# A retention layer with a gated FFN on one core: the order of all engines is replaced, and the first three FFN units become 128 tokens wide

## The chip, the cores and the metric

The kernel runs on one core of one Trainium2 chip. The metric is the device time of one execution in microseconds, and "time" below is the median of several executions. A core has TensorE (PE, matmuls, with weight loads as PEld), VectorE (DVE), ScalarE (ACT), GpSimd (POOL) and SyncE (SP), which here issues nearly all DMAs. The engines work side by side, each through its own list of instructions in order, and wait for each other with semaphores.

## The reference

Attention by a decaying state (retention), whose output is the input of an FFN with a convolved gate:

```python
# B, H, S, D = 4, 8, 768, 64;  d_model 512, d_ff 1024, three taps
gamma = 1.0 - 2.0 ** (-5.0 - np.arange(H))
for t in range(S):
    state = gamma[None, :, None, None] * state + np.einsum('bhd,bhe->bhde', k[:, :, t], v[:, :, t])
    y[:, :, t] = scale * np.einsum('bhd,bhde->bhe', q[:, :, t], state)
x = y.transpose(0, 2, 1, 3).reshape(B, S, H * D)
h = np.maximum(x @ w_in, 0.0)
conv_out = sum(conv_w[k] * hp[:, k:k + S, :] for k in range(3))   # hp: h padded by one token at each end
out = (h * 1.0 / (1.0 + np.exp(-conv_out))) @ w_out
```

All inputs are float32, and w_in, w_out and conv_w arrive as 64-bit words whose bits the kernel turns into float32 itself.

## The kernel before

The four batches are two groups of two, and a sequence is cut into 12 chunks of 64 tokens. So there are 24 **steps** n, each one chunk of one group: 2 batches, 8 heads, 64 tokens. A step has these tasks.

- `load_qk(n)`, `load_kv(n)`: 512 KB each into the buffer `rw`, of which there are four. A qk load waits until the step that had the buffer is done; the kv load of the same step waits for no buffer of its own.
- `scale_q(n)` on VectorE (L387) and the scaling of v, on ScalarE for the first steps (`scale_v_act`, L399) and on VectorE for the others (`scale_v`, L393). Both multiply by powers of gamma, from the table `gq_sb` (loaded once, 256 KB) or from `gq` tiles that ScalarE makes of it (L381).
- `scores(n)`: 16 products of 64x64 by 64x64 in f32, for steps 0 to 2 as tasks of their own. `masked(n)` (L444, VectorE) applies the causal mask.
- `mix(n)` on TensorE (L424): up to 64 such products, namely the step's outputs y (32), the state's update (16) and the scores of step n+1 (16), two of the one kind and two of the other in turn. Mix 0 has 32, mix 1 has 48.
- `carry(n)` (L452, ScalarE) copies the state for the next step; `x_head(n)` (L468, ScalarE) and `x_rest(n)` (L473, VectorE) split y into two f32r parts, which are the FFN's x; `halo` copies single columns between neighbouring units.

The FFN works in **units** of consecutive steps (`UNITS`, eight of three). A unit of three steps has 2 x 192 tokens, and with an edge column at each end of both batches its x has 388 columns. For each of eight slices f of d_ff, `mm1(u, f)` is 12 f32r matmuls (L553, three products of parts for each quarter of d_model) into `ps_m`; then `relu` (L560) and the middle tap (L568) on ScalarE, the two side taps on VectorE (L573). For each pair p of slices follow the sigmoid (L578, ScalarE), the gating (L583, VectorE) and the split of the result (L587 ScalarE, L592 VectorE). `mm2(u, t, p)` (L605) is 6 matmuls of 512 columns for 128 tokens t and pair p; the last 128 tokens of all are split into two halves of 256 columns. `put` (L613) copies to SBUF, and `out` stores.

Weights: each of the 8 + 8 pieces `w(i)` of 512 KB is loaded (`load_w`, waits for no buffer) and converted by a chain of seven tasks, `w_abs`, `w_clamp`, `w_shift`, `w_sign`, `w_bits`, `w_head`, `w_rest`, mostly on VectorE. `CONV` is the number of conv_w, which takes the first five of them.

What sets the order: `ORDER` holds a string for each engine, one letter a task (s scores, a mix, A to I mm1 of unit 0 to 8, o mm2). `plan` takes the letters in order, keeps a clock with fixed costs for tasks and loads, gives out buffers by it, and emits the tasks; each engine then runs them in just that order. The clock has one more effect: where it shows TensorE waiting for more than 0.7 us ahead of the first mm1, `keep_warm` puts dummy matmuls of 512 columns (L351) there, one for each 232 ns beyond 0.4 us; eight stand at the start in any case. The loads have eight semaphores in turn, so up to eight can be under way.

Of the kernel before, what the change touches and what calls it, by code (L numbers as in the profile page):

```python
# [27 lines left out]
CONV = 2 * NF  # L28
# [5 lines left out]
HALF = (slice(0, D), slice(D, P))  # L34


UNITS = [3, 3, 3, 3, 3, 3, 3, 3]
FIRST_STEP = [sum(UNITS[:u]) for u in range(len(UNITS))]
UNIT_OF = [u for u, w in enumerate(UNITS) for _ in range(w)]
W_MAX = max(UNITS)  # L40
LAST = (len(UNITS) - 1, UNITS[-1] - 1)


EARLY, V_ON_ACT = 2, 10

BUFS = {'rw': 4, 'xu': 3, 't2': 4, 'hc': 11, 'g': 3, 'ps_s': 1, 'ps_yo': 4, 'ps_m': 2, 'gq': 2}


ORDER = {
    "PE": (  # L50
        "sssaaaaAAaAAaAaAaBBaBABaABBBoaoaaBDCCaoDoooCCCCaoDooCooooCaDoooooDooooooDEaaoDEoDoooEoEoooEooaooEoooEFao"
        "EoooFoFaooooaoFooFoFFGFooooooGoGGaaGoooGGooHooooooHHoHoGoHoHooHoooooooooHoooooooooooooo"
    ),
    "DVE": (
        "qqmcqmmhgbqcrhgcbmqhrrlqrlgcbhgmqlbchlmcghbcglbmhqrgcqlbmcrhhgrgbqblyymyzzmqcchqgbyhvlyzvgdcybqmylzzlrre"
        "hzdgzbmrvrqmcelrdyvzqrhgmqyycbzdhclzhgygcyzrzybevbemcdzhhllyggqvbebydzzylzmlreyydezzydyyymqdyzzzzvydyvdq"
        "yzyyezqzdzzvrezmyydrezdyqezmzydqezyreyzzymedzdvrvyzdyevmqvqzeyyrzezmremryyzyvdzdeezyyyzzyydzyzzzeymdddry"
        "yeyyzrzeedzzdezyzyzeyyzyzzdyydzedzydyezzyezdeeyzde"
    ),
    "ACT": (  # L60
        "kavkvcaxvacwxvxcwkxchhavAwawaAaxcvwkAvAcaxwvacAxhkwhvAtcttwaaBatcBgtBvkBxAwttewAxBtxagkcgttxechaBhaBwxxB"
        "ectaDCgtwkgxtgDweaCctCwtCCCetwwxgtgetttCpptepcgCtttcDgtDghekttxtgepepgheDkgDttpEcxcDxDeEtttEegttegEppthc"
        "gxeEgthpEEFtetxcEFextctepgptxhgFFFehFFpettctttFtppGgpeGttGGgcggexxttGteeGgGgHepHtpHGtettHHtgHtgtegetpHtg"
        "eegtppepHtgepppp"
    ),
    "Pool": (
        "xxxxxxxx"
    ),
    "DMA": (
        "qqgwqvvqwvwvqwqvqwvwwqvqwwvqvwwqwqvvvwwqqwvwvwqqvqvvqvooqoqvoqvqvqvooovooqvoooooooooooooooo"  # L70
    ),
}

# [1 line left out]
LETTER = {  # L75
# [5 lines left out]
}  # L81
# [6 lines left out]
def letter(k):  # L88
    if k[0] in ("mm1", "relu"):
        return chr(ord("A") + k[1])  # L90
    return LETTER[k[0]][k[3] // 2 if k[0] == "conv_side" else 0]


# [20 lines left out]
def list_tasks():  # L114
# [14 lines left out]
    for n in range(N_STEPS):  # L129
        c, u = n % NC, UNIT_OF[n]  # L130
        first, width = FIRST_STEP[u], UNITS[u]
        own, both = n <= EARLY, EARLY < n + 1 < N_STEPS
# [37 lines left out]

    for u, width in enumerate(UNITS):
        n0, n1 = FIRST_STEP[u], FIRST_STEP[u] + width
# [35 lines left out]
def plan(tasks):  # L208

    queues = {engine: {} for engine in ORDER}  # L210
    for k, t in tasks.items():
        queues[t[0]].setdefault(letter(k), []).append(k)
# [473 lines left out]
```

## Time and profile before

| | before |
|---|---|
| time, median of 3 runs | 357.53 us (354.54 to 358.0) |
| the profiled execution, its time | 357.53 us |
| its span | 355.8 us |
| TensorE busy, matmuls | 341.0 us (96%), 4349 |
| VectorE busy | 220.8 us (62%) |
| ScalarE busy | 193.3 us (54%) |
| keep-warm matmuls | 37, 13.5 us busy |
| moved by DMA | 40.83 MB, 33.91 read |

The span is the time from the first to the last instruction that the profiler recorded; the execution's own time is 1.73 us longer. A group of instructions has its busy time, the mean of one in nanoseconds, and the idle time of the engine just ahead of it with what ended it. Matmuls overlap in time, so the mean of one is more than its share of the time; where the pace of a run of matmuls is needed, it is read from the chain, which gives start and duration of each run. "issue" is a wait that no semaphore, engine or DMA in the profile explains.

### The profile page before, as it was taken

Reading aid. Unit: us, or ns where it says so; the run is one execution under the profiler, and the core shown is the slowest. Engines: PE = TensorE matmul, PEld = TensorE weight load, DVE = VectorE, ACT = ScalarE, POOL = GpSimd, SP = SyncE. Lnnn points to the kernel's source line nnn. Section 1 sums busy time; section 2 is a strip of 40 time slices with the busy share of each in tenths; the row PEclk is TensorE's granted clock in tenths of the full one; section 3 lists DMA queues with packets and bytes.
Section 4 is the critical chain, followed back from the end, with each engine's and each line's share of the span. In section 5 each row is a group of like instructions: output and inputs, shape, how many; then the busy total and the mean of one; then the engine's idle time right before and its main releaser. Section 6 shows DMA issues by size and latency. Waiting matters only on the chain.

```text
span 355.8 us, 9805 instructions
## 1 busy us (share of the span) xinstructions
PE 341.0 (96%) x4349; PEld 304.5 (86%) x4349; DVE 220.8 (62%) x363; ACT 193.3 (54%) x390; POOL 1.9 (1%) x10
## 2 busy tenths in 40 slices
PE   8789959999999999998999999999999999999994
PEld 6678859998999989887988888889989988998883
DVE  1677956899999959966057745344516831188530
ACT  2865939788657565775163541343627631177422
POOL 1000000000000000000000000000000000000000
PEclk9989999999999999999999999999999999999999
DMA  7979666864830017004300633020020000100202
GB/s 292 412 263 358 214 226 216 320 247 171 298 123 0 4 38 196 34 31 123 117 2 0 186 142 122 2 61 2 29 59 33 0 2 29 29 2 29 88 2 89
DMA packets 13338, 40.83 MB, mean 115 GB/s; under 512 B 1744, under 2 KB 2000, under 8 KB 13296
## 3 DMA queue, kind: packets, MB, share of 16 engines
q1 hardware_dynamic: 13232, 40.14, 32.4%
q8 instruction: 34, 0.56, 0.7%
q0 software_dynamic: 64, 0.07, 0.1%
q14 instruction: 8, 0.07, 0.1%
HBM read 33.91 MB, written 6.29 MB: 113 GB/s over the span
## 4 chain that ended last, share of the span: by engine, by line
PE 96%; issue 2%; DVE 0%; ACT 0%
PE ps_m L553 39%; PE ps_yo L605 38%; PE ps_s L424 6%; PE ps_yo L424 5%; PE ps_st L424 4%; PE ps_yo L351 3%; DVE rw L444 0%; ACT rw L452 0%; ACT t L613 0%; DVE warm L344 0%
## 5 line engine op out<-in xcount | busy, mean ns | idle before, releaser
L553 PE MATMUL ps_m<-xu,w 128*128 128x388 f32 x768 | 144.8, 342 | 1.6 <-issue 1.6
L553 PEld LDWEIGHTS ps_m<-xu,w 128*128 128x128 f32 x768 | 136.8, 189 | 5.8 <-issue 2.1
L605 PE MATMUL ps_yo<-w,g 128*128 128x512 f32 (+1 forms) x600 | 140.2, 386 | 0.0
L605 PEld LDWEIGHTS ps_yo<-w,g 128*128 128x128 f32 x600 | 108.5, 188 | 21.7
L573 DVE SCALAR_TENSOR_TENSOR hc<-hc,cw_sb,hc 128x384 f32<-128x384 f32 x128 | 74.1, 615 | 35.7 <-ACT hc L568 35.4
L560 ACT ACTIVATE hc<-ps_m 128x388 f32<-128x388 f32 x64 | 31.5, 493 | 57.9 <-PE ps_m L553 57.9
L424 PE MATMUL ps_yo<-rw 64*64 64x64 f32 x1472 | 50.3, 223 | 6.3 <-issue 6.3
L424 PEld LDWEIGHTS ps_yo<-rw 64*64 64x64 f32 x1472 | 46.7, 138 | 6.9 <-issue 6.9
L592 DVE TENSOR_TENSOR g<-hc,g 128x768 fp32r<-128x768 f32 x32 | 30.5, 955 | 22.7 <-ACT g L587 22.6
L583 DVE TENSOR_TENSOR hc<-hc,hc 128x768 f32<-128x768 f32 x32 | 30.5, 955 | 14.6 <-ACT hc L578 14.6
L578 ACT ACTIVATE hc<-hc 128x768 f32<-128x768 f32 x32 | 26.9, 845 | 19.8 <-DVE hc L573 19.8
L568 ACT ACTIVATE hc<-hc,cw_sb 128x384 f32<-128x384 f32 x64 | 37.5, 614 | 0.1
L444 DVE TENSOR_TENSOR rw<-ps_s,mask_sb 128x512 f32<-128x512 f32 x24 | 16.6, 690 | 31.9 <-PE ps_s L424 31.9
L587 ACT CAST g<-hc 128x768 fp32r<-128x768 f32 x32 | 26.6, 833 | 14.4 <-PE ps_yo L605 11.5
L424 PEld LDWEIGHTS ps_s<-rw 64*64 64x64 f32 x768 | 24.3, 134 | 7.0 <-issue 5.3
L613 ACT COPY t<-ps_yo 128x512 f32<-128x512 f32 (+1 forms) x25 | 14.2, 568 | 27.1 <-PE ps_yo L605 26.1
L424 PE MATMUL ps_s<-rw 64*64 64x64 f32 x768 | 27.6, 221 | 0.3
L424 PE MATMUL ps_st<-rw 64*64 64x64 f32 x704 | 25.7, 221 | 0.7 <-ACT rw L452 0.7
L424 PEld LDWEIGHTS ps_st<-rw 64*64 64x64 f32 x704 | 23.1, 137 | 1.0 <-ACT rw L452 0.8
L468 ACT CAST xu<-ps_yo 128x512 fp32r<-128x512 f32 x24 | 14.2, 594 | 15.5 <-PE ps_yo L424 12.6
L473 DVE TENSOR_TENSOR xu<-ps_yo,xu 128x512 fp32r<-128x512 f32 x24 | 16.3, 687 | 7.5 <-ACT xu L468 7.4
L452 ACT COPY rw<-ps_st 128x512 f32<-128x512 f32 x22 | 12.9, 587 | 13.4 <-PE ps_st L424 8.9
(30 smaller groups left out, 149.3 us busy)
## 6 DMA issues: line engine op xcount, KB each, us to landing
rw<-in_qk SPq DMA_DIRECT2D x24, 512.0 KB, 4.0
rw<-in_kv SPq DMA_DIRECT2D x24, 512.0 KB, 5.8
w<-in_w_in SPq DMA_DIRECT2D x8, 512.0 KB, 7.3
w<-in_w_out SPq DMA_DIRECT2D x8, 512.0 KB, 6.7
out_y<-t SPq DMA_DIRECT2D x15, 256.0 KB, 2.0
out_y<-t SPq DMA_DIRECT2D x18, 128.0 KB, 2.4
gq_sb<-in_gq SPq DMA_DIRECT2D x1, 256.0 KB, 5.0
gvf_sb<-in_gvf POOLq DMA_DIRECT2D x1, 36.0 KB, 4.3
```

Of the source, the lines that this page charges most:

```text
L424: nc.tensor.matmul(out, lhsT, rhs, start=start, stop=stop, skip_group_check=True)
L444: nc.vector.tensor_tensor(out=heads_of(n)[:, 1], in0=s_of(n), in1=mask_sb.unsqueeze(1).unsqueeze(1).broadcast_to([P, G, NPAIR, C]), op=ALU ...
L473: nc.vector.tensor_tensor(out=lo, in0=y_of(n), in1=hi.bitcast(F32), op=ALU.subtract)
L553: nc.tensor.matmul(buf("ps_m", (u, f))[:, :n], w[:, k], x[:, k], start=(i == 0), stop=(i == len(products) - 1))
L560: nc.scalar.activation(h, buf("ps_m", (u, f))[:, : G * (UNITS[u] * C + 2)], AF.Relu)
L568: nc.scalar.activation(cv, h, AF.Copy, scale=w)
L573: nc.vector.scalar_tensor_tensor(out=cv, in0=h, scalar=w, in1=cv, op0=ALU.mult, op1=ALU.add)
L578: nc.scalar.activation(cv, cv, AF.Sigmoid)
L583: nc.vector.tensor_tensor(out=cv, in0=h, in1=cv, op=ALU.mult)
L587: nc.scalar.copy(g_of(u, p)[:, 0], cv_of(u, 2 * p))
L592: nc.vector.tensor_tensor(out=lo, in0=cv_of(u, 2 * p), in1=hi.bitcast(F32), op=ALU.subtract)
L605: nc.tensor.matmul(ps, g, w[:, cs], start=(f == 0 and i == 0), stop=(f == NF - 1 and i == 2))
```

## The change

`UNITS` becomes two, two, two and then six of three steps: nine units, the first three with 2 x 128 tokens, or 260 columns of x. `V_ON_ACT` goes from 10 to 8, so v of steps 8 and 9 is scaled by VectorE. The strings of all engines are new. `letter` gives the tasks of conv_w letters of their own, so that a string can place them apart from the other weights. Buffers, costs and code of the tasks stay as they are; the lines behind `letter` move down by two.

```diff
-UNITS = [3, 3, 3, 3, 3, 3, 3, 3]
+UNITS = [2, 2, 2, 3, 3, 3, 3, 3, 3]
...
-EARLY, V_ON_ACT = 2, 10
+EARLY, V_ON_ACT = 2, 8
...
     "PE": (
-        "sssaaaaAAaAAaAaAaBBaBABaABBBoaoaaBDCCaoDoooCCCCaoDooCooooCaDoooooDooooooDEaaoDEoDoooEoEoooEooaooEoooEFao"
...
+        "sssaaaaAAAaAAaAABBBBBAaBBCCoCBaCCoaCoCaoCooooDDaaDoooaaoDooDaoDooDEoaoEDoEEaooooaoooEooEoooooEooEFaFFFFF"
...
     "DMA": (
-        "qqgwqvvqwvwvqwqvqwvwwqvqwwvqvwwqwqvvvwwqqwvwvwqqvqvvqvooqoqvoqvqvqvooovooqvoooooooooooooooo"
+        "qgqwqwvvqwvwvqwqcwvwqvqwqwqvwwwvwwvvwwqqqvvqovovqqvqvqvoqvqvoqvooqovoovqvqoovoooooooooooooo"
...
 def letter(k):
     if k[0] in ("mm1", "relu"):
         return chr(ord("A") + k[1])
+    if k[1:] == (CONV,) and (k[0] == "load_w" or k[0].startswith("w_")):
+        return {"load_w": "c", "w_abs": "z"}.get(k[0]) or LETTER[k[0]].upper()
     return LETTER[k[0]][k[3] // 2 if k[0] == "conv_side" else 0]
```

TensorE's first instructions, before (keep-warm matmuls write `ps_yo<-warm`; the rows of `ps_s` are the scores of steps 0, 1 and 2, those of `ps_st` and the second `ps_yo` the start of mix 0):

```order
L351 MATMUL ps_yo_74<-warm 128x512 x8
L351 MATMUL ps_yo_111<-warm 128x512 x12
L424 MATMUL ps_s_124<-rw_85 64x64 x16
L351 MATMUL ps_yo_146<-warm 128x512 x2
L424 MATMUL ps_s_149<-rw_87 64x64 x16
L351 MATMUL ps_yo_174<-warm 128x512 x2
L424 MATMUL ps_s_177<-rw_92 64x64 x16
L424 MATMUL ps_st<-rw_85 64x64 x2
```

and of the changed kernel:

```order
L353 MATMUL ps_yo_74<-warm 128x512 x8
L353 MATMUL ps_yo_107<-warm 128x512 x6
L426 MATMUL ps_s_114<-rw_85 64x64 x16
L353 MATMUL ps_yo_140<-warm 128x512 x2
L426 MATMUL ps_s_143<-rw_88 64x64 x16
L353 MATMUL ps_yo_173<-warm 128x512 x5
L426 MATMUL ps_s_179<-rw_92 64x64 x16
L353 MATMUL ps_yo_209<-warm 128x512 x5
L426 MATMUL ps_st<-rw_85 64x64 x2
```

Six keep-warm matmuls fewer stand ahead of the first scores, three more ahead of the third and five ahead of mix 0. Further on, 3, 3 and 7 stood ahead of mix 2, mix 3 and the first mm1; now 7 and 5 stand ahead of mix 2 and mix 3, and none ahead of mm1.

The SP queue's first loads, before (`rw<-in_qk` and `rw<-in_kv` are the loads of steps, `w<-in_w_in` those of pieces 0 to 7, `gq_sb` the decay table):

```order
L361 DMA rw_85<-in_qk 128x1024
L361 DMA rw_87<-in_qk 128x1024
L369 DMA gq_sb<-in_gq 128x512
L498 DMA w_90<-in_w_in 128x1024
L361 DMA rw_92<-in_qk 128x1024
L365 DMA rw_85<-in_kv 128x1024
L365 DMA rw_87<-in_kv 128x1024
L361 DMA rw_100<-in_qk 128x1024
L498 DMA w_108<-in_w_in 128x1024
L365 DMA rw_92<-in_kv 128x1024
```

and of the changed kernel:

```order
L363 DMA rw_85<-in_qk 128x1024
L371 DMA gq_sb<-in_gq 128x512
L363 DMA rw_88<-in_qk 128x1024
L500 DMA w_90<-in_w_in 128x1024
L363 DMA rw_92<-in_qk 128x1024
L500 DMA w_98<-in_w_in 128x1024
L367 DMA rw_85<-in_kv 128x1024
L367 DMA rw_88<-in_kv 128x1024
L363 DMA rw_133<-in_qk 128x1024
L500 DMA w_136<-in_w_in 128x1024
```

The table goes up one place, a second weight piece comes ahead of the first kv, and 13 loads, not 12, stand ahead of the first that waits for a buffer.

The SP queue from the load of q and k of step 9, which waits for mix 5's buffer, before (`w<-in_w_out` are pieces 8 to 15):

```order
L361 DMA rw_769<-in_qk 128x1024
L365 DMA rw_638<-in_kv 128x1024
L498 DMA w_777<-in_w_out 128x1024
L498 DMA w_780<-in_w_out 128x1024
L361 DMA rw_875<-in_qk 128x1024
```

and of the changed kernel:

```order
L363 DMA rw_795<-in_qk 128x1024
L367 DMA rw_420<-in_kv 128x1024
L500 DMA w_801<-in_w_out 128x1024
L500 DMA w_817<-in_w_out 128x1024
L500 DMA w_823<-in_w_out 128x1024
L367 DMA rw_526<-in_kv 128x1024
L500 DMA w_830<-in_w_out 128x1024
L500 DMA w_847<-in_w_out 128x1024
L367 DMA rw_672<-in_kv 128x1024
L367 DMA rw_795<-in_kv 128x1024
L500 DMA w_876<-in_w_out 128x1024
L500 DMA w_880<-in_w_out 128x1024
```

Where three loads followed that one ahead of the next wait for a buffer, eleven follow now: seven weight pieces and four kv.

More of the change, by code (lines that the diff above doesn't have):

```diff
@@ L50 @@
     "PE": (
-        "sssaaaaAAaAAaAaAaBBaBABaABBBoaoaaBDCCaoDoooCCCCaoDooCooooCaDoooooDooooooDEaaoDEoDoooEoEoooEooaooEoooEFao"
-        "EoooFoFaooooaoFooFoFFGFooooooGoGGaaGoooGGooHooooooHHoHoGoHoHooHoooooooooHoooooooooooooo"
+        "sssaaaaAAAaAAaAABBBBBAaBBCCoCBaCCoaCoCaoCooooDDaaDoooaaoDooDaoDooDEoaoEDoEEaooooaoooEooEoooooEooEFaFFFFF"
+        "aoooFoFoooooaGGGGoooooGGaooooGoGHoaoHoHoooHooHoHooooaHooHIooIIIoooIooooIIooIooooooooooooooooooo"
     ),
     "DVE": (
-        "qqmcqmmhgbqcrhgcbmqhrrlqrlgcbhgmqlbchlmcghbcglbmhqrgcqlbmcrhhgrgbqblyymyzzmqcchqgbyhvlyzvgdcybqmylzzlrre"
@@ L56 @@
-        "hzdgzbmrvrqmcelrdyvzqrhgmqyycbzdhclzhgygcyzrzybevbemcdzhhllyggqvbebydzzylzmlreyydezzydyyymqdyzzzzvydyvdq"
-        "yzyyezqzdzzvrezmyydrezdyqezmzydqezyreyzzymedzdvrvyzdyevmqvqzeyyrzezmremryyzyvdzdeezyyyzzyydzyzzzeymdddry"
-        "yeyyzrzeedzzdezyzyzeyyzyzzdyydzedzydyezzyezdeeyzde"
+        "qqmqmchgcmhgbbqlcrhglbcrhmqrgcbmhllrqgcbhcmlhgCbqgHblGBlyrqzcmhqcgyhybgyzlrcbdhyzzzgrcybzlylechhmgycvdhg"
+        "bzmbcdzglhqbecqhlgvmrecblghbdlgyblelrzrmqyvyzyydvyqemzzyzvqdzmvredqryeymqyvzzzyydzzdyrzyrdmeeqyqyvzzyzzz"
@@ L59 @@
+        "yvzydemddyyyzmyzzedqzreqzyrzeyvzdmyedrqzdeyzyvezvqdmeryyymzyzyzdreyzzmryzvydzyeyvyyedzrmdzzzvzqeeddyyezy"
+        "ymzzrezdvyqdyzyzyzdyezezmydrzeeydyzeyzrzyzyyzzddeedyyzezdyzyyzyzyzeddeyzzede"
     ),
     "ACT": (
-        "kavkvcaxvacwxvxcwkxchhavAwawaAaxcvwkAvAcaxwvacAxhkwhvAtcttwaaBatcBgtBvkBxAwttewAxBtxagkcgttxechaBhaBwxxB"
-        "ectaDCgtwkgxtgDweaCctCwtCCCetwwxgtgetttCpptepcgCtttcDgtDghekttxtgepepgheDkgDttpEcxcDxDeEtttEegttegEppthc"
-        "gxeEgthpEEFtetxcEFextctepgptxhgFFFehFFpettctttFtppGgpeGttGGgcggexxttGteeGgGgHepHtpHGtettHHtgHtgtegetpHtg"
@@ L64 @@
-        "eegtppepHtgepppp"
+        "kakavvwcaxvwacxvxcahkhwwzxcAavaAwAkcvwxAwAthcAahxtAaBttBtBwagBavtaAwBxettBhhgwBgavCkCceCaBCwwcxeagwCtcxC"
+        "awtwextCtwcthphtCgpteDcxgtkxtetgDtetktctgcxxgDgeteDttcktpDgtDkptegtDgEtectexEDgtgexEttEgexpcepgtEkctxegp"
+        "EettephhEEhttpFxcFtgFeFttgtFthxFFgtFttceGeGxgGtgpgepepGthcteGtGxghgttGcGttgeHxtepHgteHtcppHegtHHtexHgtHt"
+        "ptgpIItIeIepgteIgIttttegItgIepptepgepppp"
     ),
     "Pool": (
-        "xxxxxxxx"
+        "xxxxxxxxx"
     ),
```

## The prediction

> **What bounds the kernel now.** First the page: the share of the engines, the granted clock, the instruction queue, the chain's shares, and four groups.
>
> ```profile
> span 355.8 us, 9805 instructions
> ...
> PE 341.0 (96%) x4349; PEld 304.5 (86%) x4349; DVE 220.8 (62%) x363; ACT 193.3 (54%) x390; POOL 1.9 (1%) x10
> ...
> PEclk9989999999999999999999999999999999999999
> ...
> q8 instruction: 34, 0.56, 0.7%
> ...
> PE 96%; issue 2%; DVE 0%; ACT 0%
> ...
> L553 PE MATMUL ps_m<-xu,w 128*128 128x388 f32 x768 | 144.8, 342 | 1.6 <-issue 1.6
> ...
> L573 DVE SCALAR_TENSOR_TENSOR hc<-hc,cw_sb,hc 128x384 f32<-128x384 f32 x128 | 74.1, 615 | 35.7 <-ACT hc L568 35.4
> ...
> L583 DVE TENSOR_TENSOR hc<-hc,hc 128x768 f32<-128x768 f32 x32 | 30.5, 955 | 14.6 <-ACT hc L578 14.6
> ...
> L444 DVE TENSOR_TENSOR rw<-ps_s,mask_sb 128x512 f32<-128x512 f32 x24 | 16.6, 690 | 31.9 <-PE ps_s L424 31.9
> ```
>
> TensorE is the path, 96% of it. No other engine holds it; the only named rest is "issue", time in which it waited for nothing that the profile shows. So I read the chain in order of time (start, duration, what), to see where that stands.
>
> ```profile
> 9.02 1.10 PE ps_s L424 x32
> ...
> 15.60 0.27 PE ps_st L424 x2
> 16.40 1.09 issue
> ...
> 25.84 1.05 issue
> ...
> 29.96 4.41 PE ps_m L553 x24
> ...
> 43.60 1.58 issue
> ...
> 48.83 3.02 issue
> ...
> 52.43 3.54 PE ps_m L553 x12
> ...
> 103.02 2.13 PE ps_m L553 x12
> ...
> 162.00 0.20 PE ps_s L424 x2
> 165.60 1.17 issue
> ...
> 337.01 14.02 PE ps_yo L605 x84
> 351.05 0.37 ACT t L613
> ```
>
> Five stalls, 7.9 us together, four of them before 52 us. The 34 packets of queue q8 explain them: 4349 matmuls and 4349 weight loads are 8698 instructions, 256 to a packet. A 64x64 f32 product runs as two matmuls with a load each, so it takes four instructions, and 64 products fill a packet; counted this way, with the few waits that are instructions of their own, each of the five stalls stands where a packet begins. When do packets travel? The DMA view for 164 to 165 us, and for 49.5 to 49.6 us:
>
> ```profile
> DMA packets 1, 0.02 MB, mean 16 GB/s; under 512 B 0, under 2 KB 0, under 8 KB 0
> ...
> q8 instruction: 1, 0.02, 7.0%
> ```
>
> ```profile
> q1 hardware_dynamic: 10, 0.04, 99.4%
> q8 instruction: 1, 0.02, 60.2%
> ```
>
> At 164 us the packet is the only transfer there is, and TensorE still stands until 166.77, some 2.4 us after it began to move. From 162.00 to 165.60 run 114 products of mixes 16 and 17, 31.6 ns each, so a packet of products alone is used up in 2.0 us. It ended in a stall of 1.17: the next packet is asked for about when one begins, and from there to its first matmul go 3.2 us on idle queues. In the second case the packet moves 2.3 us before the stall ends at 51.84, but it can have been asked for at 45.2, when the stall before ended. In between it lay behind four loads of 512 KB:
>
> ```profile
> 43.00 0.33 SPq L361 DMA_DIRECT2D rw<-in_qk  x1
> 43.37 0.76 SPq L365 DMA_DIRECT2D rw<-in_kv  x1
> 44.17 0.90 SPq L498 DMA_DIRECT2D w<-in_w_out  x2
> ```
>
> Their rate is read from two arrivals, the decay table (two loads and its own half) and the first kv (5.5 loads), three loads apart in 3.87 us, 1.29 us a load:
>
> ```profile
> 6.67 1.28 ACT L381 ACT_TABLE_LOAD   x1 [6.67 <-DMA gq_sb<-in_gq]
> ...
> 10.54 1.28 ACT L399 ACTIVATE rw<-rw,gvf_sb 128x128 f32<-128x128 f32 x4 [0.73 <-DMA rw<-in_kv]
> ```
>
> So **an instruction packet stands in line behind the loads issued before it.** The Trainium skill, "Runtime: NRT & Kernel Launch", section "Instruction fetch mechanics", says that the fetch is mostly hidden, because dispatch is slower than the refill; this trace does not agree, with 7.9 us in the open.
>
> A stall costs a second time. TensorE's busy time (the second number) and granted clock (the third from the end) in stretches of 3.4 us:
>
> ```profile
> 14.10:17.50 3.40, 1.62 (x94) 1.34 (x85) 3.33 (x7) 2.61 (x8) 0.00 (x0) 1.00 1.03 407
> 17.50:20.90 3.40, 3.40 (x61) 3.19 (x62) 2.51 (x5) 2.51 (x7) 0.00 (x0) 0.50 0.77 300
> ...
> 48.20:51.60 3.40, 0.63 (x42) 0.49 (x35) 2.28 (x6) 0.00 (x0) 0.00 (x0) 1.00 0.68 265
> 51.60:55.10 3.50, 3.26 (x19) 3.14 (x19) 1.22 (x3) 2.72 (x9) 0.00 (x0) 0.51 0.46 133
> ```
>
> ```profile
> 24.30:27.70 3.40, 2.35 (x116) 1.84 (x118) 2.36 (x4) 2.39 (x7) 0.00 (x0) 1.00 0.84 261
> ```
>
> After a stretch busy for 1.62 or 0.63 us the clock is half for the next; after one busy for 2.35 it stays whole. The price is in the chain: twelve mm1 matmuls took 3.54 us at 52.43 and 2.13 at 103.02, 1.4 more, about 1.7 with the rest of the mix beside them. The Trainium skill, "TensorE: Matmul & The Clock Gate", Part 1, has the same window of 3.4 us, but asks for a whole idle one; here a half idle one was enough.
>
> **The change part by part, against this execution's span of 355.8 us** (its time, 357.53, is 1.73 more and is also the median of the three runs).
>
> *Narrow units.* mm1 becomes 288 matmuls of 260 columns and 576 of 388: 384 columns more in all, and 96 matmuls more. A matmul of 388 takes 2.13/12 = 0.177 us. The row at 337.01 holds 36 of 512 columns and 48 of 256: at 0.2315 for 512 the 48 take 14.02 - 8.33 = 5.69, 0.1185 each, so a weight load doesn't bound them, and a column is 0.44 ns with some 6 ns a matmul beside. 96 x 6.5 ns + 384 x 0.44 ns = **+0.8 us**, all on the path. VectorE gets sixteen more L573, sixteen more of the kinds of L583 and two scale_v. L583 and L444 differ by 256 columns and 0.265 us, which leaves 0.16 us beside the columns, and 0.22 for L573: 3.5 + 2.6 + 2 x 0.69, about 7 us. VectorE is busy 62% and TensorE never waits for it, so I cost this at nothing; with that cover gone it is up to 7. ScalarE, at 54%, loses two scale_v for as many small pieces: nothing.
>
> *The front, up to the first mm1.* Six keep-warm matmuls fewer, 0.23 us each, bring the first scores 1.4 us ahead of 9.02. It is lost again. kv(0) is the 6.5th load, no longer the 5.5th: it lands at 11.8, its scaling takes 1.28, the first mix starts at 13.2. The second waits for ScalarE's carry, now behind w_head(0), until about 15.7 (15.60 before). The packet that begins in mix 2, at product 29, is asked for at 16 us, behind every load through w(4), 14.5 of them. By arrivals a load count n has landed at 3.4 + 1.29n; the bytes have gone some 0.9 earlier, so 2.5 + 14.5 x 1.29 = 21.2, and 2.4 later it is in use, 23.6; mix 2 needs it at 20. The one that begins in mix 3 is asked for then, behind w(6), the 18.5th: 26.4, in use at 28.8, mix 3 ends at 30.0 and mm1 starts at 30.2. One row speaks against so strict a line:
>
> ```profile
> 7.98 0.33 SPq L365 DMA_DIRECT2D rw<-in_kv  x1
> ```
>
> This was the last of 11.5 loads; a packet behind it would move at 17.3, and that of the stall at 16.40 moved 2.4 before the stall's end at 17.49, at 15.1. With 2 us in line at most, both times, mm1 starts at 27.3; if the line is 1 us longer, at 31.2. I take 29.6, nearer to the line, against 29.96: **-0.4 us**, from -2.7 to +1.2.
>
> *From there to mm1(1,6).* Before: 1.58 + 3.02 us of stalls, and 1.7 of half clock. After, mm1 tasks go ahead of mixes 4 and 5, and one stall stays, at the end of mix 5: the packet ahead holds nine mm1 matmuls and 59 products, 2.95 us, and two loads issued at the end of mix 4 are still in line, 0.6 us of them: 3.2 + 0.6 - 2.95 = 0.9. Then comes a release. The end of mix 5 frees a buffer, and the SP queue issues twelve loads with no further buffer to wait for: 12 x 1.29 = 15.5, 1.3 to the first byte and 2.4 from packet to matmul, so a packet asked for meanwhile is in use 19.2 after mix 5. TensorE gets to it through eight mm1 tasks of 1.45, a mix of 2.2 and 21 matmuls of 0.121, at 16.4: a stall of 2.8, in mm1(1,6). Stalls 3.7 against 4.6, **-0.9 us**. The half clock goes, **-1.7**, unless one 3.4 us stretch holds most of that stall, then 0; the edges of the stretches cut it as they fall, and I take -1.7.
>
> *Later.* Before, one packet lies wholly inside a pair of mixes, 16 and 17: 1.17. After, two do, in 10 and 11 and in 12 and 13, each begun 35 products deep, with nothing wide to read ahead of: 2 x (3.2 - 2.0) = 2.4, **+1.2 us**; 2.2 each if a load is in line.
>
> Sum: 0.8 - 0.4 - 0.9 - 1.7 + 1.2 = **-1.0 us**: span 354.8, time **356.5 us**.
>
> **Rivals.** *The packets are hardly late (faster).* For it: the row at 7.98, and that the mixes wait for loads at 13 and 19 us in any case, which covers part of a packet. Front -2.7, both middle stalls gone (-4.6), half clock gone, the rest as above: -7.0, time 350.5.
>
> *The burst after mix 5 (slower).* Place: mm1(1,6). Mechanism: the twelve loads at once ahead of its packet. Price: at 1.5 us a load it moves 2.5 later, the stall is 5.3 and half clock follows; with the front at its high end and 2.2 for each late stall that is 0.8 + 1.2 + (0.9 + 5.3 - 4.6) + 0 + 3.2 = +6.8, time 364. It decides from a stall of 3.7 us on, and from 2.0 on where half clock follows it: there the sum turns positive. Against it: the longest line seen, before 49.5, was some 4 us.
>
> *VectorE becomes the wait.* From 100 to 150 us it is nearly as full as TensorE, 45.5 of 50:
>
> ```profile
> 100.00:150.00 50.00, 50.00 (x576) 45.06 (x568) 45.50 (x78) 31.59 (x60) 0.00 (x0) 1.00 0.23 70
> ...
> 57.87 0.62 DVE L573 SCALAR_TENSOR_TENSOR hc<-hc,cw_sb,hc 128x384 f32<-128x384 f32 x1 [1.31 <-ACT hc L568]
> ```
>
> If half of its 7 us shows, the time is 360. Against it: its first conv work, at 57.87 here, can start once unit 0 has two steps, not three, and conv_w comes nine places earlier.
>
> *The stalls are not packets.* Then the issue time has another cause and stays, and only the wide work changes: 358.3. That is what the Trainium skill, "Runtime: NRT & Kernel Launch", section "Instruction fetch mechanics", would have. The view at 164 us, one packet alone and a stall that ends behind it, speaks against it.
>
> **How the numbers follow.** A measurement of this kernel can hardly tell less than 1% (3.6 us) from no change, and my walk through the start is good to 3 us. Forecast, within 1%: 0.40. Packets hardly late, faster: 0.34. Burst, slower: 0.12. VectorE: 0.09, half of it slower by over 1%. Not packets, within 1%: 0.05. With 0.01 from the forecast's low edge that makes faster 0.35, same 0.48, slower 0.17. The forecast's own range is 353.5 to 360; the range reaches down to the first rival and up past VectorE's price into the burst: 350 to 361.5.
>
> **What would show it.** In the chain of the changed kernel: issue pieces inside mixes 2, 3 and 5, one of about 2.8 us inside an mm1 near 60 us, two of about 1.2 between mixes 10 and 13; the first mm1 at 29.6; granted clock whole from 31 us on; twelve 260-column matmuls in 1.45 us. An mm1 before 28 us would mean that packets don't wait as I say. TensorE waiting for VectorE or ScalarE after 60 us would break the claim that nothing else holds it; then the forecast is low.

## The result, and the profile after

| | before | after |
|---|---|---|
| median of 20 runs | 356.76 us (353.6 to 359.48) | 358.2 us (355.57 to 360.98) |
| ratio, 95% interval | | 1.0053 (1.0031 to 1.0074) |
| the profiled execution, its time | 357.53 us | 358.47 us |
| its span | 355.8 us | 356.7 us |

The changed kernel is 0.5% slower. The ratio leaves out the executions marked as slow (360.98 and 360.95 us of the changed kernel among them) and so is not the quotient of the two medians, 1.004. The forecast was 356.5 us, a little faster. The execution that the sum was made against is itself 0.8 us above its kernel's median over 20 runs; the spans of the two profiled executions differ by 0.9 us, where the forecast had -1.0.

The page of the changed kernel, the same rows as before (busy time and share of the span of each engine; the granted clock; the instruction queue; the chain's shares):

```profile
span 356.7 us, 10053 instructions
PE 341.6 (96%) x4446; PEld 304.8 (85%) x4446; DVE 225.8 (63%) x389; ACT 195.7 (55%) x408; POOL 1.9 (1%) x10
PEclk9998999999999999999999999999999999999999
q8 instruction: 35, 0.57, 0.7%
PE 90%; ACT 3%; issue 2%; DMA 2%; DVE 1%; SPq 0%; DVEq 0%; ACTq 0%
```

TensorE is still the path, but its share of the chain fell from 96 to 90%: ScalarE, DMA and VectorE now have pieces in it. Pieces of the chain in order of time (start, duration, what):

```profile
16.41 0.49 ACT rw L454
16.95 0.27 PE ps_st L426 x2
22.28 1.60 issue
27.46 1.95 issue
31.28 5.52 PE ps_m L555 x36
43.80 0.67 issue
53.79 1.28 ACT L580
62.63 0.72 issue
89.09 5.60 PE ps_yo L607 x24
102.19 1.05 issue
114.40 0.79 issue
352.50 0.37 ACT t L615
```

The issue pieces stand where the prediction put them: in mixes 2, 3 and 5, in mm1(1,6), and two between mixes 10 and 13. They sum to 6.8 us against 7.9 before. Counted over TensorE's recorded instructions (matmuls, weight loads and waits, in order of their start), the number ahead of the matmul that ends a stall is 193 or 194 past a multiple of 256 for all eleven stalls of the two kernels. Three things are new. The first mm1 starts at 31.28, not at 29.96. ScalarE's piece of 1.28 us at 53.79 is in the chain. And the mm2 row has 24 matmuls in 5.60 us, 1.400 for a task of six, where the kernel before has

```profile
255.21 8.36 PE ps_yo L605 x36
```

1.393 for a task. The stretches around the first mm1, cut where the granted clock changes in this trace, every 3.41 us (second number TensorE's busy time, third from the end its granted clock), and the place of the half clock of before:

```profile
26.68:30.09 3.41, 1.46 (x97) 1.32 (x92) 1.64 (x4) 2.73 (x10) 0.00 (x0) 1.00 0.86 339
30.09:33.51 3.42, 3.42 (x57) 3.30 (x46) 3.42 (x7) 1.08 (x2) 0.00 (x0) 0.50 0.36 114
51.60:55.10 3.50, 3.50 (x30) 3.34 (x28) 3.50 (x9) 2.81 (x6) 0.00 (x0) 1.00 1.01 408
```

The half clock of before (51.6 to 55.1) is gone, but the stall in mix 3 leaves a stretch busy for only 1.46 us, and the half clock behind it starts at 30.09. The first mm1 pays 1.2 us: its 36 matmuls take 5.52 us where three tasks of 1.446 (an undisturbed task of 260 columns) would take 4.34. The rest of mix 3, from 30.09 to 31.28, pays some 0.6 more. The granted clock was whole from 33.51 on, not from 31 on as forecast.

### The profile page after: what moved, and what is told of

It is laid out like the page before. It is cut to its first block, busy times and chain, and to the rows that moved or that the text cites. A ratio compares the mean times of both kernels' runs of the same rounds, so it can differ in the third digit from the quotient of the medians.

```text
span 356.7 us, 10053 instructions
## 1 busy us (share of the span) xinstructions
PE 341.6 (96%) x4446; PEld 304.8 (85%) x4446; DVE 225.8 (63%) x389; ACT 195.7 (55%) x408; POOL 1.9 (1%) x10
## 4 chain that ended last, share of the span: by engine, by line
PE 90%; ACT 3%; issue 2%; DMA 2%; DVE 1%; SPq 0%; DVEq 0%; ACTq 0%
PE ps_yo L607 38%; PE ps_m L555 38%; PE ps_s L426 5%; PE ps_yo L426 4%; PE ps_st L426 4%; DMA rw<-in_qk 2%; PE ps_yo L353 1%; ACT t L504 0%; ACT w L540 0%; DVE t L521 0%; ACT L580 0%; ACT hc L562 0%; ACT rw L401 0%; DVE t L514 0%; SPq L363 0%
## 5 line engine op out<-in xcount | busy, mean ns | idle before, releaser
L555 PE MATMUL ps_m<-xu,w 128*128 128x388 f32 (+1 forms) x864 | 145.1, 323 | 1.7 <-ACT hc L562 0.9
L555 PEld LDWEIGHTS ps_m<-xu,w 128*128 128x128 f32 x864 | 138.5, 190 | 5.4 <-ACT hc L562 1.3
L575 DVE SCALAR_TENSOR_TENSOR hc<-hc,cw_sb,hc 128x384 f32<-128x384 f32 (+1 forms) x144 | 77.2, 570 | 43.1 <-ACT hc L570 42.9
L562 ACT ACTIVATE hc<-ps_m 128x388 f32<-128x388 f32 (+1 forms) x72 | 32.9, 457 | 62.3 <-PE ps_m L555 60.8
L594 DVE TENSOR_TENSOR g<-hc,g 128x768 fp32r<-128x768 f32 (+1 forms) x36 | 31.1, 866 | 27.5 <-ACT g L589 27.4
L570 ACT ACTIVATE hc<-hc,cw_sb 128x384 f32<-128x384 f32 (+1 forms) x72 | 40.2, 577 | 0.4 <-DVE hc L585 0.3
L589 ACT CAST g<-hc 128x768 fp32r<-128x768 f32 (+1 forms) x36 | 27.3, 760 | 22.2 <-PE ps_yo L607 19.3
L580 ACT ACTIVATE hc<-hc 128x768 f32<-128x768 f32 (+1 forms) x36 | 27.9, 775 | 14.7 <-DVE hc L575 14.6
L585 DVE TENSOR_TENSOR hc<-hc,hc 128x768 f32<-128x768 f32 (+1 forms) x36 | 30.9, 864 | 7.0 <-ACT hc L580 7.0
L426 PEld LDWEIGHTS ps_s<-rw 64*64 64x64 f32 x768 | 24.5, 134 | 8.3 <-issue 6.5
```

The costliest lines, as they stand in the source:

```text
L426: nc.tensor.matmul(out, lhsT, rhs, start=start, stop=stop, skip_group_check=True)
L555: nc.tensor.matmul(buf("ps_m", (u, f))[:, :n], w[:, k], x[:, k], start=(i == 0), stop=(i == len(products) - 1))
L562: nc.scalar.activation(h, buf("ps_m", (u, f))[:, : G * (UNITS[u] * C + 2)], AF.Relu)
L570: nc.scalar.activation(cv, h, AF.Copy, scale=w)
L575: nc.vector.scalar_tensor_tensor(out=cv, in0=h, scalar=w, in1=cv, op0=ALU.mult, op1=ALU.add)
L580: nc.scalar.activation(cv, cv, AF.Sigmoid)
```

## The experiments

The theory: an instruction packet waits behind loads that were issued before it, and a packet that holds only products of 64x64 is used up before the next is there; the changed kernel is slower because its start has more loads ahead of the packets of mixes 2 and 3, with smaller losses on ScalarE and in mm2. The rivals: the stalls come with the mixes themselves (data, semaphores, pairs), or the chain through VectorE and ScalarE to x sets the start. All ratios are to the kernel before on the same chip (medians 356.26, 357.15 and 355.43 us on the three chips used); 1.0053 is the changed kernel's. The changed kernel itself was not run again beside the experiments, so a difference from 1.0053 also holds what chips differ in. In the strings of the DMA queue q is a load of q and k, v of k and v, w of a weight piece, c of conv_w.

### Two loads fewer ahead of mix 3's packet

```diff
-        "qgqwqwvvqwvwvqwqcwvwqvqwqwqv...
+        "qgqwqwvvqwvwvqwqcvqwwvqwqwqv...
```

> The changed kernel with two weight loads moved: pieces 5 and 6 of w_in are issued behind the q and k load of step 6 instead of ahead of it, nothing else. Theory (instruction packets stand in line behind the loads issued before them): the packet that begins in mix 3 has two loads fewer ahead of it, 16.5 instead of 18.5, so it moves near 24.2 us instead of 26.80; the stall in mix 3 falls from 1.95 us to at most 0.3, the half clock in the first mm1 goes, the first mm1 starts near 29.3 instead of 31.2, and the whole is 2 to 3 us shorter. Rival (the stall has a cause in the mix itself, data or semaphores): stall and time stay. Second rival (VectorE's and ScalarE's chain to x sets the start of mm1): the stall falls, but TensorE then waits for x and mm1 stays at 31.

Measured: 357.28 us, ratio 1.0017 (0.9986 to 1.0047), profiled span 354.7. The chain:

```profile
21.82 1.69 issue
28.51 4.54 PE ps_m L555 x36
40.95 1.24 issue
```

The stall of 1.95 in mix 3 is gone, mm1 starts 2.8 us earlier and runs its first 36 matmuls nearly at full pace. A DMA view shows the packet of mix 3 moving at 24.5 to 24.7 (forecast 24.2), with hardly a load beside it (16 engines' share of the loads' queue 12%):

```profile
q8 instruction: 1, 0.02, 35.0%
q1 hardware_dynamic: 7, 0.01, 12.2%
```

That is the theory, and both rivals fall. By the end of its first 36 matmuls the run is 3.7 us ahead, 1.0 of it gained in these matmuls. But 0.9 us was lost again up to mix 5, with a new stall of 0.38 in mix 4 (33.43), and 0.6 at the end of mix 5, where the stall grew from 0.67 to 1.24. Why it grew is not shown. In the ten traces of the changed order and its variants that stall ran from nothing to 2.10 us, with 1.5 to 1.7 loads in line each time the packet ahead began. The span fell by 2.0 us, the ratio by 0.36%, which the runs alone barely tell from nothing.

### ScalarE's carry ahead of the weight

```diff
-            "kakavvwcaxvw...
+            "kakavvcwaxvw...
```

(The keep-warm matmuls ahead of mix 2 were held at seven, as in the changed kernel.)

> The changed kernel with ScalarE's first carry ahead of the head of weight piece 0, which it stood behind (it waited there until 16.4 us). Theory (the packet line sets the front): mix 1 starts 0.5 to 1.5 us earlier, but the packet of mix 2 moves at 21.3 as before, so the stall in mix 2 (1.60) grows by as much as mix 1 gains and the first mm1 stays within 0.4 us of 31.2; time the same. Rival (ScalarE's chain sets the front): the gain of mix 1 reaches mm1, start near 30, time 1 us shorter.

Measured: 357.68 us, ratio 1.0038 (1.0002 to 1.0073).

```profile
16.23 0.27 PE ps_st L427 x2
17.02 1.27 issue
22.79 1.20 issue
31.30 5.62 PE ps_m L556 x36
```

Mix 1 starts 0.7 earlier (16.23 against 16.95) and mm1 0.02 later. The gain went into a stall of 1.27, though in mix 1 and not in mix 2 as expected: a packet that begins there had been covered by the wait for the carry. ScalarE's carry does not set the start; the packets do.

### The table of the sigmoid at the start

```diff
+    nc.scalar.activation(const.tile([P, 1], F32, name="early"), warm.bitcast(F32)[:, :1], AF.Sigmoid)
```

In the changed kernel ScalarE loads the table ahead of the first sigmoid, and TensorE waits for the relu behind it (matmuls of mm1(1,4), start and duration, with the wait ahead of them):

```profile
56.04 1.71 PE L555 MATMUL ps_m<-xu,w 128*128 128x260 f32 x12 [0.89 <-ACT hc L562]
```

> The changed kernel with one small sigmoid on ScalarE at the start, so that the table of the sigmoid may be there before its first use; the result is the same. Theory: no 1.28 us table load near 54 us, TensorE's wait for relu in mm1(1,4), 0.89 us, goes. But the packet of mm1(1,6) is set by the burst of loads behind mix 5 and still moves near 60.8, so the stall there grows from 0.72 to about 1.6 and the time stays within 0.5 us. Rival (the two waits are independent): the time is 0.9 us shorter and the stall stays 0.7.

Measured: 356.31 us, ratio 0.9996 (0.9963 to 1.0028), span 354.5. The wait is gone, and the theory as I had put it is wrong:

```profile
43.66 11.75 PE ps_m L556 x96
57.45 2.81 PE ps_m L556 x21
60.27 0.77 issue
```

The stall stayed at 0.77. The packet moved at 58.6, 2.2 us earlier than in the changed kernel, though the same twelve loads stood ahead of it. Of these, 1.2 us come from mix 5, whose end releases the loads and was that much earlier (first load issued at 43.78, in the changed kernel at 44.95); 0.9 us remain. A DMA view of 58.6 to 58.8 shows it among loads at full rate:

```profile
q1 hardware_dynamic: 26, 0.08, 103.3%
q8 instruction: 1, 0.02, 32.2%
```

So the line is not strict. Counted from the bytes issued and moved, 4.7 loads were in line when the packet ahead began to run, 3.4 when this one moved, 2.9 us later. In the changed kernel it was 3.0 loads, 1.9 left, 2.8 us. In mix 2 it took 3.2 to 3.7 us with 2.9 to 3.4 loads in line, and with less than one load 0.6 to 1.7, mostly near 1.1. A packet passes part of a long line; by which rule, the runs do not show. The start of the packet ahead is also only a stand-in for the moment of asking: in the changed kernel one packet moved at 36.59, 0.4 us before the one ahead of it began. The stall of 0.67 at the end of mix 5 is gone in this run too, since its packet moved at 39.6, not 41.7. The edit does not touch that place, so I take that part for chance.

### Eight loads at once instead of twelve

```diff
-...qwqvwwwvwwvvwwqqqvv...
+...qwqvwwwvwwqvvwwqqvv...
```

> The changed kernel with the q and k load of step 10 (which waits for a buffer) issued four places earlier, ahead of the last two kv loads and the last two weight loads of the burst behind mix 5: eight loads go at once instead of twelve. The runs so far suggest that a packet asked for behind three or more whole loads moves about 2.9 us later, and behind an empty line 1.1 later. Theory (the burst's loads hold up the packet of mm1(1,6)): it is asked for at 58.0, the eight loads are through by about 56, so it moves near 59.1 instead of 60.78, the stall of 0.72 goes, time 0.7 shorter. Rival (the delay of that packet doesn't hang on the line): packet near 60.8, stall 0.7, time the same.

Measured: 356.65 us, ratio 0.9985 (0.995 to 1.002). The group of the narrow mm1 matmuls, in the changed kernel and here (busy time, mean ns, idle time ahead of them and what ended it):

```profile
L555 PE MATMUL ps_m<-xu,w 128*128 128x260 f32 x288 | 38.1, 290 | 1.7 <-ACT hc L562 0.9 <-issue 0.7
```

```profile
L555 PE MATMUL ps_m<-xu,w 128*128 128x260 f32 x288 | 38.3, 291 | 1.0 <-ACT hc L562 0.9
```

The issue wait of 0.7 is gone; the packet moved at 58.2, 0.2 us after the packet ahead began to run. The burst does hold it up, by 2.6 us, of which 0.7 showed. The ratio fell by 0.7%, 2.4 us, more than that stall explains; the profiled spans differ by 0.9 us.

### A wide task between the mixes of a pair

```diff
-...ooooDDaaDoooaaoDoo...
+...ooooDDaDaoooaoaDoo...
```

> The changed kernel with one task of the FFN put between mixes 10 and 11 (mm1(3,2), which came right behind mix 11) and one between mixes 12 and 13 (mm2 that came right behind mix 13). Theory (a packet that holds only products of 64x64 is read faster than the next one arrives): the packets that begin 35 products deep in mixes 10 and 12 now hold 3.9 and 3.2 us of work instead of 2.0; the stalls of 1.05 and 0.79 us fall to 0 to 0.2 and the time by 1.6 to 1.8. Rival (the stalls belong to the second mix of a pair, to its data): they stay, time the same.

Measured: 355.66 us, ratio 0.9978 (0.9944 to 1.0011). Between 95 and 118 us the chain has no issue piece over 0.3 us any more, so the two late stalls are packets of products alone. The Trainium skill, "Runtime: NRT & Kernel Launch", section "Instruction fetch mechanics", gives 256 instructions for a packet; that count is what placed the boundaries here, and the trace agrees. That the crossing is mostly hidden holds only where the packet ahead has some 3 us of work. At the end of mix 5 this run stalls for 1.82: its first mm1 started at 30.25, a microsecond earlier than in the changed kernel without an edit at that place, and the gain was lost again there.

### The place of the operands

Tiles are placed in order of first use. In the kernel before, g and w (the two operands of mm2) lay 0 or 96 bytes past a multiple of 128; in the changed kernel g lay 32 or 96 bytes past one, and w 0, 32 or 64. Placing the buffers `hc`, whose 3104 bytes shift what follows, ahead of the others gives all these tiles the same remainder (the pad is 24 elements, and 32 in the third run):

```diff
+    for i in range(BUFS["hc"]):
+        pool.tile([P, sizes["hc"]], F32, name=f"hc_{i}", bufs=1)
+    pool.tile([P, 24], F32, name="pad")
```

> The changed kernel with every tile that a matmul reads placed at a multiple of 128 bytes in a partition (the buffers hc, 3104 bytes each, are placed first, then 96 bytes of padding); instructions and order are the same. In both kernels the tiles' order of first use places them; in the changed one g lies 32 or 96 bytes past a multiple of 128 and w mostly 64. Theory (the pace of the 512-column matmuls hangs on the place of their operands; in the kernel before they took 0.2305 us where both lie on a multiple and up to 0.2327 elsewhere, in the changed kernel 0.2332): mm2 of 512 columns falls from 1.400 to about 1.383 us, 92 of them, 1.5 us less. Rival (the slower pace comes with the order, not the place): 1.400 as it was, time the same.

> The kernel before with every tile that a matmul reads at a multiple of 128 bytes, as was done with the changed kernel, where mm2 of 512 columns went from 1.400 to 1.364 us. Theory (place alone sets the pace): from 1.391 to 1.364 here too, 92 of them, 2.5 us less, near 354. With the place equal, the changed kernel's share of 0.9 us in mm2 is gone, and the two aligned kernels should differ by about 0.5 us. Rival (the aligned pace goes with the changed order): 1.391 stays.

> The changed kernel with the same placement as in the aligned run, but 32 bytes further: every operand of a matmul now lies 32 bytes past a multiple of 128. One look, for the pace of mm2 alone. If what counts is that the two operands lie alike, mm2 of 512 columns stays at 1.364 us. If a multiple of 64 or 128 bytes itself counts, it goes back to 1.390 to 1.400, the pace without the edit.

One piece of mm2 from the chain of each, the changed kernel aligned, the kernel before aligned, and the changed kernel with all operands 32 bytes further:

```profile
89.42 5.45 PE ps_yo L610 x24
```

```profile
150.86 8.20 PE ps_yo L608 x36
```

```profile
92.29 5.47 PE ps_yo L610 x24
```

A task of six takes 1.363, 1.367 and 1.368 us in these pieces, against 1.400 and 1.393. Over all tasks the gain is smaller: the busy time of the 552 matmuls of 512 columns falls from 136.1 to 133.6 us in the changed kernel and from 134.8 to 133.3 in the kernel before, 2.5 and 1.5 us, where I expected 1.5 and 2.5. The pace goes with the placement, not with the order. It does not need a multiple of 128, since 32 bytes further it is the same. Nor is it enough that g and w lie alike. Matched with the program's addresses, the ten tasks of the changed kernel with both operands 32 bytes past a multiple took 1.398 us each, the other groups of its tasks 1.394 to 1.401; and 25 tasks of the kernel before with both on a multiple took 1.383 (median), against 1.360 aligned. What else the new places bring is open. The times: 355.68 us, 0.9984 (0.995 to 1.0018) for the changed kernel; 354.84 us, 0.9968 (0.9936 to 1.0001) for the kernel before; one run of the third, 358.94 beside 358.29 for the kernel before. The ratios fell by 0.7 and 0.3%, near the 2.5 and 1.5 us, but their intervals are as wide. In the aligned changed kernel's profile (the chain, then stretches of 3.41 us) mix 5's stall is 2.10 and costs a half clock:

```profile
42.00 2.10 issue
```

```profile
41.92:45.33 3.41, 1.31 (x23) 1.17 (x17) 2.65 (x5) 1.24 (x4) 0.00 (x0) 1.00 0.00 0
45.33:48.75 3.42, 3.42 (x18) 3.42 (x17) 1.09 (x3) 2.04 (x5) 0.00 (x0) 0.50 0.97 317
```

With the place equal the two kernels differ by 0.16% of the time instead of 0.53%. That is what I expected, but each of the two intervals reaches 0.34% to either side.

### The loads of the kernel before

```diff
-...wwqvqwwvqvwwqwqvvvww...
+...wwqvqwwvqvqwwwqvvvww...
```

> The kernel before, with two weight loads (pieces 8 and 9) issued behind the q and k load of step 10 instead of ahead of it, nothing else. Theory (packets in line behind loads): the packet behind the stall of 3.02 us at 48.83 has two loads fewer in front, so it moves near 47 instead of 49.57; the stall falls to about 0.4, the stretch of half clock behind it (51.6 to 55.1) goes, 1.3 to 1.7, together 3.5 to 4.5 us less: near 352.5. Rival (the stall has another cause than the line): stall, half clock and time stay as they are. In between, if other loads take the place of the two: stall near 3, time the same.

Measured: 354.42 us, ratio 0.9946 (0.9915 to 0.9978). The chain, and the stretches around the second stall, again cut where this trace's clock can change:

```profile
42.64 0.51 issue
46.79 1.65 issue
```

```profile
47.42:50.84 3.42, 2.40 (x22) 2.32 (x21) 1.54 (x4) 2.02 (x6) 0.00 (x0) 1.00 0.30 75
50.84:54.25 3.41, 3.41 (x135) 3.11 (x134) 2.16 (x6) 3.41 (x12) 0.00 (x0) 1.00 0.99 364
```

The largest stall of the kernel before falls from 3.02 to 1.65, not to 0.4, and the half clock goes. The packet moved at 46.05, a microsecond before the forecast, but TensorE stood there 2.0 us earlier (46.79 against 48.83): mm1 had begun 1.0 us earlier, at 28.98, with no edit in front of it, and the stall before was 0.51, not 1.58. Over the runs the edit gave 1.9 us, half of the 3.5 to 4.5 expected; the profiled run, the fastest of the ten, shows 4.6. With the aligned places added:

> The kernel before with both: the two weight loads behind the q and k load of step 10, and all matmul operands at multiples of 128 bytes. If the two gains are independent, 2.5 us and 1.9 us (what the loads gave over several runs; the one profiled run of it gave 4.6): near 352. If the faster mm2 only lets TensorE reach its waits sooner, less than the sum.

Measured: 352.41 us, 0.9909 (0.9875 to 0.9944), near the 352 of independent gains.

### Together

The five edits of the changed kernel in one, and the same with mm1(0,5) ahead of mix 5:

```diff
-        "sssaaaaAAAaAAaAABBBBB...
+        "sssaaaaAAAaAAAaABBBBB...
```

> The changed kernel with the five edits tried one by one: two weight loads behind the q and k load of step 6, the sigmoid's table loaded at the start, eight loads instead of twelve behind mix 5, a wide task between mixes 10 and 11 and between 12 and 13, operands at multiples of 128 bytes. Independent gains would add up to 2.7 (first mm1 near 28.5) + 0.9 + 0.7 + 1.8 + 3.3 = 9.4 us: near 349. But in each run where the first mm1 came earlier the stall at the end of mix 5 grew (0.67 to 1.24 and 2.04), since its packet stands behind the two loads issued behind mix 4; by that 1 to 2 us come back there, near 350.5.

> As the run with five edits, and with mm1(0,5) ahead of mix 5 instead of behind it. Theory (a packet of products alone): the packet ahead of the one that stalls at the end of mix 5 then holds 4.1 us of work instead of 2.9, and the stall there falls by about 1.2 us against the run with five edits, the time likewise. Rival (that stall comes with the mix itself or its loads): no difference between the two.

Measured: 349.99 us, 0.9828 (0.979 to 0.9866), and 350.04 us, 0.9843 (0.9803 to 0.9882). The first is near the 350.5 that I expected with part of the gain lost again. Both beat the kernel before, by 1.7 and 1.6%, and the changed kernel by 2.2 and 2.1% of its time. The first has its stall at mix 5, the second lost it and waits there for the weight (0.55 us) and for relu (0.50):

```profile
41.27 1.25 issue
```

```profile
35.08 0.60 DVE w L549
39.19 0.70 DVE w L549
```

So the stall is a packet's, as the theory had it, but a new wait took its place, and the time did not move.

## Why the prediction was wrong

By its own steps, from the two profiled executions (us):

| step | forecast | measured |
|---|---|---|
| narrow units | +0.8 | +0.8 |
| start of the first mm1 | -0.4 | +1.3 |
| middle stalls | -0.9 | -3.2 |
| half clock | -1.7 | -0.2 |
| late stalls | +1.2 | +0.7 |
| TensorE waiting for relu | 0 | +0.9 |
| pace of mm2, 92 tasks | 0 | about +0.8 |
| after the last matmul | 0 | -0.55 |
| sum | -1.0 | +0.55; the spans differ by +0.9 |

0.35 us is spread over small pieces that I did not place. The misses partly cancel, and that is luck: start, half clock, relu and mm2 came out 4.9 us worse than forecast, the stalls and the end 3.3 better.

**The start is the step that failed.** The prediction's line gave 30.2 for the first mm1, and I took 29.6, since one packet of the kernel before seemed not to have waited. The packets moved at 21.34 and 26.80, a little behind the line's 21.2 and 26.4; the second was in use at 29.42, not 28.8, and the half clock in the rest of mix 3 took the 0.6 us that are left to 31.28. So the line from the first bytes was nearly right, and leaving it for 29.6 was wrong. The first mix was late as well, at 14.08 us and not at 13.2, because kv(0) landed at 12.77 and not at 11.8:

```profile
12.77 2.56 ACT L401 ACTIVATE rw<-rw,gvf_sb 128x128 f32<-128x128 f32 x8 [0.58 <-DMA rw<-in_kv]
```

That part probably cost nothing by itself: in the run with the carry, 0.7 us gained ahead of mix 2 is lost to the packets. The start measured my stated high end, +1.2, and the run with two loads fewer began mm1 2.8 us earlier. One pair of profiles would not prove that, since the start varies by a microsecond and more with nothing changed ahead of it. But the traces keep apart: 28.98 to 30.13 in the four of the kernel before, 30.25 to 32.81 in the seven with the changed kernel's first loads, 28.30 to 28.82 in the three with the two loads moved.

**The half clock was mis-sized** because I looked for it where the kernel before has it and in mm1(1,6), not at the start. The row counts mm1 alone; the 0.6 us in mix 3 are in the start. It depends on where the stretches fall: of those seven traces, four have all of the first mm1's beginning at half clock, one a part of it (0.8 us), two none.

**The burst was right in place and wrong in size**: a stall in mm1(1,6), 0.72 for 2.8. The prediction counts both sides from the end of mix 5, so a late start moves both and does not matter. From that end (44.86) the packet was in use after 18.5 us, not 19.2, and TensorE was there after 17.8, not 16.4: 0.9 of that is the wait for relu, the rest slightly longer tasks. The table run, in which the packet moved 15.0 us after that end and not 15.9, shows that it does not wait for all twelve loads; that it came near the forecast here was chance. That also takes the ground from the burst rival, whose price grew with the whole line.

**Not in the sum at all**: the wait for relu, where the prediction has "nothing" for ScalarE. The table load ran at 65.5 us in the kernel before, for the same 1.28 us, where nothing waited; with narrow units the first sigmoid comes at 53.8, among mm1 tasks of 1.45 us that each need a relu. And the place of the tiles, which a new order changes without a word in the diff.

Right were the narrow units, VectorE's cover (5.0 us more busy, no wait of TensorE for the conv work; the 7 us forecast counted sixteen more pieces of the kinds of L583 where the pages show eight), the places of all six stalls, and that packets set the start. The rival "the stalls are not packets" is out: moving two loads, or one task, removes a stall.

## What to carry to other kernels

Where stalls stand that the profile ends with "issue", count instructions. Here a boundary came every 256 of them, and TensorE stalled where the packet ahead held less work than the next one took: some 3 us with a nearly empty queue, up to 6.7 with three loads in it (45.18 to 51.84 in the kernel before). A wide task between the narrow ones, or a load issued two places later, removed such a stall. A gain ahead of such a boundary was often lost again there, so edits have to be tried together: five that gave 0.36 to 0.75% each against the changed kernel's 1.0053, 3.0% by addition, gave 2.2% in one. When an order is replaced, look also at what moves silently: where the tiles lie, and when an activation table is loaded for the first time.

## What the runs showed of the hardware that was not expected

- The placement of the tiles in SBUF changes the pace of the 512-column matmuls by 1 to 2%: the group is busy for 2.5 us less in the changed kernel (first fence, then the same aligned) and 1.5 us less in the kernel before (last fence: as it was, then aligned). The matmuls of 388 columns did not gain (mean 339 ns in both profiles of the changed kernel).

```profile
L607 PE MATMUL ps_yo<-w,g 128*128 128x512 f32 x552 | 136.1, 397 | 0.0
L555 PE MATMUL ps_m<-xu,w 128*128 128x388 f32 x576 | 107.1, 339 | 0.0
```

```profile
L610 PE MATMUL ps_yo<-w,g 128*128 128x512 f32 x552 | 133.6, 393 | 0.0
L558 PE MATMUL ps_m<-xu,w 128*128 128x388 f32 x576 | 107.0, 339 | 0.0
```

```profile
L605 PE MATMUL ps_yo<-w,g 128*128 128x512 f32 x552 | 134.8, 395 | 0.0
L608 PE MATMUL ps_yo<-w,g 128*128 128x512 f32 x552 | 133.3, 392 | 0.0
```

- An instruction packet passes part of the loads ahead of it: in two runs it moved 2.8 and 2.9 us after the start of the packet ahead, with 3.0 and 4.7 loads in line. It is no fixed time: in the kernel before the packet of 49.57 took 4.4 us with 3.3 loads.
- In all 14 traces the granted clock changes only on a grid of 3.41 us. Between the first recorded change and 345 us, eleven stretches of this grid that had the whole clock were followed by one of half clock; TensorE was busy in them for 0.36 to 1.63 us. The least busy one that stayed whole had 1.70 (in the run with a wide task between the mixes), so half of a stretch, 1.71, is near the border. One stretch already at half clock and busy for 2.62 us was followed by another half one (the kernel before, aligned). The least busy whole one, and the stretch behind it:

```profile
14.72:18.13 3.41, 1.70 (x96) 1.51 (x87) 2.83 (x6) 2.50 (x6) 0.00 (x0) 1.00 1.03 407
18.13:21.55 3.42, 3.42 (x87) 2.75 (x83) 3.19 (x7) 3.31 (x9) 0.00 (x0) 1.00 1.03 410
```
